# The first step's v one place earlier in the load queue, and one weight pair asked for at the state's sum

## The chip, the cores and the metric

The kernel runs on one core of one Trainium2 chip. The metric is the device time of one execution in microseconds; the median of several runs is compared. Five engines work side by side, each through its own list of instructions in order: TensorE (PE; its weight loads are listed apart as PEld), VectorE (DVE), ScalarE (ACT), GpSimd (POOL), and SyncE (SP), which here only starts DMA transfers.

## The reference

Two blocks follow each other. The first is a recurrent attention over 768 time steps, for 4 batches and 8 heads of dimension 48:

```
for t in range(S):
    cur = einsum('bhd,bhe->bhde', u * k_t, v_t)
    y[:, :, t] = einsum('bhd,bhde->bhe', r_t, state + cur)
    state = w_t[..., None] * state + einsum('bhd,bhe->bhde', k_t, v_t)
```

The second takes the result as 3072 tokens of 384 numbers and runs `h = x @ w_in` (384 to 2048), `g = h * erf(softplus(h))`, and `out = g @ w_out` (2048 to 384). The weights `w_in` and `w_out` come as 64-bit floats; everything else is 32-bit.

## The kernel before

The sequence is cut into chunks of 128 tokens, and two batches go together, so there are 12 steps (6 chunks times 2 batch pairs). In every step the attention of the chunk is computed in six levels. At each level TensorE multiplies blocks of k and r (`level_products`, L554), VectorE multiplies r and k by running products of the decay w (`scale`, L323 and L330), and the block's result is taken into a tile `own` (L564, or L571 on ScalarE at level 6). Then `from_own` (L586) multiplies `own` with v into the PSUM tile `y`, `state_part` (L661) makes k times v, `through_state` (L612) adds what comes from the carried state, and the chunk's output is copied to `xT`. The second block of an earlier step is interleaved: `hidden` (L1021) makes the products with `w_in` in pieces, each of which ScalarE copies out of PSUM (L1030, two PSUM buffers `m`), and `project` multiplies with `w_out`.

The weights are converted on the chip, in the first three steps. They are cut into 16 pairs: 0 to 7 of `w_in`, 8 to 15 of `w_out`. Each pair is loaded as 32-bit words into one of three buffers named `words` (two DMAs, L147), scaled by ScalarE twice (high words L257 or L259, low words L265), shifted by VectorE (L274), and finished by an addition on GpSimd (L287). Piece n of the first hidden layer needs pair n. The functions are kept in a table by letter: "l" load, "b" and "r" ScalarE's two scalings, "h" the shift, "o" the addition, "j" shift and addition. `done` counts how far each letter has come, and the table `CONVERT` lists, by step and level, which letters are sent: the first string of an entry before the level's result is taken, the second after it.

The order of every engine's list is the order in which the program is written (a manual schedule). When a load may start is set by a gate: a one-element copy into the buffer that is about to be loaded, which reads something that comes late enough. The DMA then waits for the copy. The copy runs on GpSimd (L242) or, where told so, on ScalarE (L240). All these loads are started by SP, in order, so a load whose gate is closed holds back everything behind it.

Two places matter here. In step 0, at level 2 of `attend_first`, SP gets pair 1's load with a gate (L800), then the first step's v (L801), then step 1's w (L802). v is read by `from_own(0, own, 1)`. In step 1, the state after step 0 is made late, in `pending()`: `state_part` on TensorE, then VectorE's two additions into `S_next` (L854). It leaves `S_next` in `turns["gate"]`, and the next load without a gate of its own takes it from there. That is pair 5's load, sent after level 2 by `("j", "brl")`; by then pair 3's shift and addition ("j") have been sent, so on GpSimd the gate copy stands behind pair 3's addition. Behind pair 5 SP has step 2's r and k (`load_halves(loaded[2][0], rkw[2])`), then pairs 6 and 7.

Of the kernel before, what the change touches and what calls it, by code (L numbers as in the profile page):

```python
# [61 lines left out]
def kernel(  # L62
# [14 lines left out]
    nc = tc.nc  # L77
# [51 lines left out]
    turns = {"next": 0}  # L129

    def products(shape, n=None):


        if n is not None:
            return ps_p.tile(shape, FP32, name=f"pp{n}")
        n = turns["next"]
        turns["next"] = 1 - n
        return ps_p.tile(shape, FP32, name=f"pp{n}")
# [5 lines left out]
    def load_halves(dst, src):  # L144

        for i in range(2):
            nc.sync.dma_start(out=dst[:, i], in_=src[:, i])  # L147
# [71 lines left out]
    def convert(weights):  # L219

        held = {}
        plain = weights[0][1].dtype == FP32
        signed = len(weights) // 2

        def load(i, behind=None, by_scalar=False):
            if i >= len(weights):
                return
            dst, src = weights[i]  # L230
            if plain:
                nc.sync.dma_start(out=dst, in_=src)
                return
            words = wide.tile([P, 2, DM, 2], I32, name="words", bufs=3)
            if behind is None:
                behind = turns.pop("gate", None)
            if behind is not None:
                to = words[:, 0, 0, 0:1].bitcast(FP32)
                if by_scalar:
                    nc.scalar.copy(to, behind)  # L240
                else:
                    nc.gpsimd.tensor_copy(out=to, in_=behind)  # L242
            load_halves(words[:].rearrange("p i n two -> p i (n two)"), src.bitcast(I32))
            held[i] = {"words": words}

        def scale_high(i, part=slice(0, 2)):


            if i not in held:
                return  # L250
            if i < 2:
                base = ps_m.tile([P, NP * C], FP32, name="m")[:, :DM]
            else:
                base = y[:].rearrange("p e q j t -> p e (q j t)")[:, :, :DM]
            high = held[i]["words"][:, part, :, 1].bitcast(FP32)
            if i < signed:
                nc.scalar.activation(base, high, AF.Prelu, scale=2.0**-112, alpha=-(2.0**32))  # L257
            else:
                nc.scalar.mul(out=base, in_=high, mul=2.0**-112)  # L259
            held[i].setdefault("bases", []).append((base.bitcast(I32), part))  # L260

        def scale_low(i):
            if i in held:
                rest = wide.tile([P, 2, DM], I32, name="rest", bufs=2)
                nc.scalar.mul(  # L265
                    out=rest[:], in_=held[i]["words"][:, :, :, 0].bitcast(U32), mul=2.0**-29
                )
                held[i]["rest"] = rest

        def shift(i):  # L270
            if i in held:
                base, part = held[i]["bases"].pop(0)
                into = weights[i][0].bitcast(I32)[:, part]
                nc.vector.tensor_scalar(  # L274
                    out=into if i < signed else base, in0=base, scalar1=3, scalar2=None,
                    op0=ALU.logical_shift_left,
                )
                if i >= signed:
                    nc.vector.scalar_tensor_tensor(
                        out=into, in0=held[i]["words"][:, part, :, 1], scalar=-(1 << 31),  # L280
                        in1=base, op0=ALU.bitwise_and, op1=ALU.bitwise_or,
                    )

        def add(i):
            if i in held:
                into = weights[i][0].bitcast(I32)
                nc.gpsimd.tensor_tensor(  # L287
                    out=into, in0=into, in1=held.pop(i)["rest"][:], op=ALU.add
                )

        def join(i):
            shift(i)
            add(i)

        stages = {"l": load, "b": scale_high, "r": scale_low, "h": shift, "o": add, "j": join}
        done = {"l": 5, "b": 2, "r": 2, "j": 2}

        def send(what):
            for stage in what:
                stages[stage](done[stage])  # L300
                done[stage] += 1

        return stages, send
# [10 lines left out]
    def scale(s, level, batch=None):  # L314

        in_t, tots = loaded[s][0], ready[s][1]
        half, nb = 1 << (level - 1), JP * C >> level
        if batch is not None:
            nb //= NJ
            halves = view(  # L320
                turns["first"][:, batch], half, [[NP * C - half, 2], [2 * half, nb], [1, half]]
            )
            nc.vector.tensor_mul(  # L323
                halves, halves,
                view(tots[level - 1], 2 * batch * nb, [[1, 2], [2, nb], [0, half]]),
            )
            return
        n = 1 if s > DIRECT and level == LOG else 2
        halves = view(in_t[:, 0:2], half, [[JP * C - half, n], [2 * half, nb], [1, half]])
        nc.vector.tensor_mul(  # L330
            halves, halves, view(tots[level - 1], 0, [[1, n], [2, nb], [0, half]])
        )
# [193 lines left out]
    def parts_of(s):  # L526

        c, i = divmod(s, SPC)
        in_t, vt = loaded[s]
        made, tots, tot = ready[s]  # L530
        ends = tot.rearrange("p (n h) -> p n h", h=NC)
        return c, in_t, vt, made, states[i][c % 2], states[i][1 - c % 2], ends
# [9 lines left out]
    def level_products(pp, rk, level, ns=range(NJ * NP)):  # L542

        half = 1 << (level - 1)
        m = HC if level <= MASKED else half
        for n in ns:
            for s0 in range(0, C, HC):
                for e in range(NE):
                    right = rk(0, n)[rows(e), s0 : s0 + HC]
                    to = pp[s0 : s0 + m, e, n, :]  # L550
                    if level > 1:
                        right = rights(right, half)
                        to = to[:, : HC // 2].rearrange("p (b h) -> p b h", h=half)
                    nc.tensor.matmul(  # L554
                        to, lhsT=rk(1, n)[rows(e), s0 : s0 + m], rhs=right,
                        start=True,
                        stop=True,
                    )
# [189 lines left out]
    def attend_first(xT):  # L748
# [5 lines left out]
        c, _, vt, made, S, S_next, ends = parts_of(0)  # L754
# [25 lines left out]
        behind = {3: (3,), 4: (4, 5), 5: (6,)}  # L780
        for level in range(2, LOG):
            pp = turns.pop("pp", None) or products([P, NE, JP, HC])
            for j, half in enumerate(halves):
                level_products(pp, first_pair, level, half)
                scale(0, level, batch=j)
            turns["pp"] = products([P, NE, JP, HC])
            keep_busy(turns["pp"], (DM,))
            take_level(own, pp, level)
            wait_for(1 << level - 1)
            if level == 2:  # L790
                totals(2, part=slice(batch // 2, batch))
            else:
                totals(*behind[level])
            if level == 2:
                stages["b"](0, 0)
                stages["b"](0, 1)
                stages["r"](0)
                for _ in prepare(1):
                    pass
                stages["l"](1, own[:, 0, 2:3])  # L800
                nc.sync.dma_start(out=vt[:], in_=v[0])  # L801
                nc.sync.dma_start(out=ws[1][:], in_=rkw[1][:, 2])  # L802
        totals = plan_totals(1)
        pp = turns.pop("pp")
# [45 lines left out]
        def pending():  # L850
            part = products([P, NE, JP, HC], turns["next"])[:, 0]
            state_part(0, kT, ps + [[part] * NE], (1,))
            for e in range(NE):
                nc.vector.tensor_add(S_next[rows(e)], faded[1][rows(e)], part[rows(e), :, :D])  # L854
            load_third()
            turns["gate"] = S_next[:, 0, 0:1]

        turns["pending"] = pending

# [364 lines left out]
    def run_late(s, tokens, following=None):  # L1224
# [26 lines left out]

    CONVERT = (
        (),
        (("j", "br"),) + (("j", "brl"),) * 4 + (("j", "l"), ("", ""), ("", ""), ("", "brl")),
        (("", "jbrl"),) * 4 + (("", "jl"), ("", ""), ("", ""), ("", ""), ("", "br")),
        (("", "jbr"), ("j", "br"), ("j", "")),
    )
# [19 lines left out]
    with tc.manual_schedule(  # L1277
# [3 lines left out]
        for t in (*states[0], *states[1], middle):  # L1281
# [3 lines left out]
        stages, send = convert(  # L1285
            [
                (into[:, f : f + 2, :], given[:, f : f + 2, :])
                for into, given in ((w_in_sb, w_in), (w_out_sb, w_out))
                for f in range(0, NT, 2)
            ]  # L1290
        )
# [165 lines left out]
```

## Time and profile before

| | us |
|---|---|
| median of 3 runs | 595.64 (592.7 to 596.28) |
| the profiled execution | 595.89 |
| its span | 594.1 |
| TensorE busy | 581.4 |
| VectorE busy | 436.7 |
| ScalarE busy | 360.8 |
| GpSimd busy | 272.8 |

The mean granted TensorE clock of the profiled execution is 0.996 of full speed. The kernel moves 63.24 MB in all; the loads of the first 60 us, weights and step inputs, take most of the DMA engines' time there.

A row of the timeline has the start and the duration in us, the engine, the source line, the operation, what it writes and reads, how many instructions are merged in the row, and in brackets how long the engine was idle before it and what ended that. "issue" means that the profile shows nothing that the engine waited for. SPq rows are DMA starts in SP's queue. A row by windows has the stretch, the sum, the busy time and the number of instructions of PE, PEld, DVE, ACT and POOL, then the granted clock, the busy share of the DMA engines and GB/s.

### The profile page before, as it was taken

The numbers are of one execution on the slowest core, as the hardware profiler recorded it, in microseconds if no ns is written. First come the engines' busy times: TensorE is split into PE (matmuls) and PEld (weight loads), VectorE is DVE, ScalarE is ACT, GpSimd is POOL, SyncE is SP. The second block draws the span as 40 slices with busy tenths as digits, with TensorE's granted clock in tenths as the row PEclk, the third lists the DMA queues.
The fourth block names the chain that finished last, engine by engine and source line by source line (L and its number), as shares of the span: only waits on it lengthen the run. The fifth ranks groups of instructions, "written<-read, shape, count | busy, mean of one in ns | idle before, by whom it ended". The sixth has DMA issues, their size and how long they took to land.

```text
span 594.1 us, 16635 instructions
## 1 busy us (share of the span) xinstructions
PE 581.4 (98%) x7256; PEld 499.1 (84%) x7256; DVE 436.7 (73%) x523; ACT 360.8 (61%) x474; POOL 272.8 (46%) x308
## 2 busy tenths in 40 slices
PE   8797999999999999999999999999999999999997
PEld 6586887678668767898898898898898898898997
DVE  7685696899996899799799799799799525023140
ACT  4536877726534497666666666666666664746710
POOL 4566263700488559649459459459459000000000
PEclk9998999999999999999999999999999999999999
DMA  7668362541324414334334334333331300000000
GB/s 243 196 211 332 114 237 88 217 143 19 142 51 151 81 77 159 72 108 169 72 108 169 73 108 168 73 108 133 73 108 53 73 8 28 2 20 15 1 26 28
DMA packets 54081, 63.24 MB, mean 106 GB/s; under 512 B 35160, under 2 KB 40568, under 8 KB 52984
## 3 DMA queue, kind: packets, MB, share of 16 engines
q1 hardware_dynamic: 53624, 61.98, 32.9%
q8 instruction: 57, 0.93, 0.7%
q10 hardware_dynamic: 384, 0.20, 0.1%
q14 instruction: 16, 0.13, 0.1%
HBM read 52.39 MB, written 8.69 MB: 103 GB/s over the span
## 4 chain that ended last, share of the span: by engine, by line
PE 60%; ACT 3%; issue 1%; DVE 1%; ACTq 0%; DVEq 0%
PE m L1129 28%; PE m L1021 27%; PE pp L554 2%; PE y L586 1%; PE y L612 1%; PE pp L661 1%; ACT room L977 1%; ACT L981 1%; ACT L977 1%; PE pp L1129 0%; ACTq L647 0%; ACT pp L981 0%; DVE in L330 0%; ACT y L981 0%; PE pp L674 0%
## 5 line engine op out<-in xcount | busy, mean ns | idle before, releaser
L1021 PE MATMUL m<-xT,w_in_sb 128*128 128x256 f32 x1152 | 259.1, 383 | 3.9 <-ACT h L1030 3.5
L1021 PEld LDWEIGHTS m<-xT,w_in_sb 128*128 128x128 f32 x1152 | 217.3, 191 | 35.8 <-issue 4.3
L1030 ACT COPY h<-m 128x512 f32<-128x512 f32 x96 | 55.4, 579 | 84.1 <-PE m L1021 84.0
L330 DVE TENSOR_TENSOR in<-in,tot_sb 128x1024 f32<-128x1024 f32 (+1 forms) x55 | 77.5, 1409 | 17.2 <-PE pp L554 13.7
L465 POOL TENSOR_TENSOR rk<-words 128x528 f32<-128x528 f32 (+3 forms) x28 | 42.5, 1516 | 92.1 <-DVE sums L455 81.7
L469 POOL TENSOR_TENSOR words<-words,rest 128x528 f32<-128x528 f32 (+10 forms) x77 | 78.2, 1015 | 6.0
L1053 PE MATMUL m<-w_out_sb,h 128*128 128x384 f32 x192 | 64.3, 491 | 0.0
L1053 PEld LDWEIGHTS m<-w_out_sb,h 128*128 128x128 f32 x192 | 35.7, 190 | 23.5
L1129 PE MATMUL m<-mixed,h 128*128 128x192 f32 x288 | 51.1, 331 | 0.0
L977 ACT ACT_TABLE_LOAD x36 | 46.2, 1283 | 3.0 <-issue 2.4
L1129 PE MATMUL m<-w_out_sb,h 128*128 128x192 f32 x272 | 47.5, 329 | 0.0
L1129 PEld LDWEIGHTS m<-mixed,h 128*128 128x128 f32 x288 | 46.6, 190 | 0.9
L981 ACT ACT_TABLE_LOAD x36 | 46.2, 1283 | 1.6 <-DVE room L1112 1.1
L1129 PEld LDWEIGHTS m<-w_out_sb,h 128*128 128x128 f32 x272 | 44.3, 190 | 0.4
L1129 PE MATMUL m<-w_out_sb,room 128*128 128x192 f32 x256 | 44.2, 326 | 0.0
L554 PEld LDWEIGHTS pp<-in 48*64 48x64 f32 (+1 forms) x2368 | 33.4, 126 | 11.8 <-issue 4.6
L1129 PEld LDWEIGHTS m<-w_out_sb,room 128*128 128x128 f32 x256 | 42.0, 190 | 0.0
L986 DVE TENSOR_TENSOR h<-h,y 128x1024 f32<-128x1024 f32 x17 | 20.7, 1215 | 28.3 <-ACT y L981 28.1
L404 POOL TENSOR_TENSOR tot_sb<-tot_sb 128x256 f32<-128x256 f32 (+4 forms) x50 | 36.9, 737 | 3.8
L977 ACT ACTIVATE room<-h 128x1024 f32<-128x1024 f32 x36 | 38.1, 1058 | 0.4
L986 DVE TENSOR_TENSOR h<-h,pp 128x1024 f32<-128x1024 f32 x19 | 23.1, 1214 | 19.7 <-ACT pp L981 19.7
L554 PE MATMUL pp<-in 48*64 48x32 f32 (+1 forms) x2368 | 37.1, 212 | 0.3 <-DVE in L330 0.2
(146 smaller groups left out, 823.4 us busy)
## 6 DMA issues: line engine op xcount, KB each, us to landing
in<-in_rkw SPq DMA_DIRECT2D x8, 1024.0 KB, 5.0
words<-in_moe_w_in SPq DMA_DIRECT2D x16, 384.0 KB, 6.9
words<-in_moe_w_out SPq DMA_DIRECT2D x16, 384.0 KB, 4.4
words<-in_rk_rows SPq DMA_DIRECT2D x8, 768.0 KB, 5.8
w<-in_rkw SPq DMA_DIRECT2D x11, 512.0 KB
v<-in_v SPq DMA_DIRECT2D x12, 384.0 KB, 5.6
out<-o SPq DMA_DIRECT2D x23, 192.0 KB, 2.8
in<-in_rkw SPq DMA_DIRECT2D x7, 512.0 KB, 6.0
```

The costliest lines, as they stand in the source:

```text
L330: nc.vector.tensor_mul(halves, halves, view(tots[level - 1], 0, [[1, n], [2, nb], [0, half]]))
L404: nc.gpsimd.tensor_mul(new, pair[:, :, 0], pair[:, :, 1])
L465: engine.tensor_mul(terms[n], r[:, :, n:], k[:, :, : near - n])
L469: engine.tensor_mul(k[:, :, :m], k[:, :, :m], w[:, :, n : n + m])
L554: nc.tensor.matmul(to, lhsT=rk(1, n)[rows(e), s0 : s0 + m], rhs=right, start=True, stop=True,)
L977: nc.scalar.activation(sp_room, chunks[0], AF.Softplus)
L981: nc.scalar.activation(at, sp_room, AF.Erf)
L986: nc.vector.tensor_mul(h, h, at)
L1021: nc.tensor.matmul(ps[:, ff, :], lhsT=w_in_sb[:, g * FG + f + ff, kk * P : (kk + 1) * P], rhs=xT[:, kk, :], start=kk == 0, stop=kk == KT - 1,)
L1030: nc.scalar.copy(h[:, f : f + FT, :], ps[:])
L1053: nc.tensor.matmul(ps[j][:], lhsT=gs[g][:, f, j * C : (j + 1) * C], rhs=w_out_sb[:, g * FG + f, :], start=g + f == 0, stop=g == NG - 1 and ...
L1129: nc.tensor.matmul(to, lhsT=a[:, f], rhs=b[:, f], start=start and f == 0, stop=f == FG - 1, skip_group_check=True,)
```

## The change

Two things move. In step 0, v's load is written ahead of pair 1's load. In step 1, pair 5's load is written into `pending()`, right after the two additions that make `S_next`, with `S_next` as its gate; the gate's hand-over through `turns` goes, and "l" goes from the entry that sent it, with `done["l"]` starting at 6 in its place. On GpSimd the gate copy of pair 5 now stands ahead of pair 3's addition instead of behind it. On SP v stands ahead of pair 1's two DMAs; the rest of SP's order, and the orders of TensorE, VectorE and ScalarE, are as they were.

```
             words = wide.tile([P, 2, DM, 2], I32, name="words", bufs=3)
-            if behind is None:
-                behind = turns.pop("gate", None)
             if behind is not None:
...
-        done = {"l": 5, "b": 2, "r": 2, "j": 2}
+        done = {"l": 6, "b": 2, "r": 2, "j": 2}
...
+                nc.sync.dma_start(out=vt[:], in_=v[0])
                 stages["l"](1, own[:, 0, 2:3])
-                nc.sync.dma_start(out=vt[:], in_=v[0])
                 nc.sync.dma_start(out=ws[1][:], in_=rkw[1][:, 2])
...
             load_third()
-            turns["gate"] = S_next[:, 0, 0:1]
+            stages["l"](5, S_next[:, 0, 0:1])
...
-        (("j", "br"),) + (("j", "brl"),) * 4 + (("j", "l"), ("", ""), ("", ""), ("", "brl")),
+        (("j", "br"),) * 2 + (("j", "brl"),) * 3 + (("j", "l"), ("", ""), ("", ""), ("", "brl")),
```

## The prediction

> **What bounds the kernel now.** I read the busy shares first, then who TensorE (PE) waited for in the first 65 us, then the timeline there, then the clock in half-microsecond slices.
>
> ```profile
> PE 581.4 (98%) x7256; PEld 499.1 (84%) x7256; DVE 436.7 (73%) x523; ACT 360.8 (61%) x474; POOL 272.8 (46%) x308
> ```
>
> PE is busy 98% of the span: 12.7 us idle in all. Cut into stretches, PE is idle 2.5 us in 0 to 21, 6.5 us in 21 to 65, 0.4 us in 65 to 232 and 3.2 us after that. So what happens before 65 us moves the end nearly one for one, if it moves PE. Who PE waited for there:
>
> ```profile
> PE m L1021 <- ACT h L1030: 3.3, 2, 2.2
> PE y L586 <- DMA v<-in_v: 1.0, 1, 1.0
> PE pp L661 <- issue: 0.9, 1, 0.9
> PE pp L554 <- issue: 0.7, 1, 0.7
> ```
>
> The largest wait is for ScalarE's copies (L1030) of hidden-layer products out of PSUM. The timeline shows why those copies are late (start, duration, engine):
>
> ```profile
> 21.91 0.66 PE L586 MATMUL y<-own,v 64*48 64x64 f32 x32 [1.02 <-DMA v<-in_v]
> 23.95 0.43 PE L661 MATMUL pp<-v,kT 64*48 64x48 f32 x11 [0.94 <-issue]
> ...
> 35.31 1.11 DVE L854 TENSOR_TENSOR s<-faded,pp 48x384 f32<-48x384 f32 x2
> 37.56 1.84 POOL L287 TENSOR_TENSOR w_in_sb<-w_in_sb,rest 128x768 int32<-128x768 int32 x1 [3.26 <-DVE w_in_sb L274]
> 39.34 1.19 POOL L242 COPY words<-s 128x1 f32<-128x1 f32 x1
> 40.55 0.81 SPq L147 DMA_DIRECT2D words<-in_moe_w_in  x2
> 41.47 0.84 SPq L147 DMA_DIRECT2D in<-in_rkw  x2
> 42.40 1.89 SPq L147 DMA_DIRECT2D words<-in_moe_w_in  x4
> 45.03 0.87 ACT L257 ACTIVATE y<-words 128x768 f32<-128x768 f32 x1 [5.22 <-DMA words<-in_moe_w_in]
> 46.62 0.56 ACT L1030 COPY h<-m 128x512 f32<-128x512 f32 x1
> 47.34 2.83 PE L1021 MATMUL m<-xT,w_in_sb 128*128 128x256 f32 x12 [1.07 <-ACT h L1030]
> 50.81 0.85 ACT L257 ACTIVATE y<-words 128x768 f32<-128x768 f32 x1 [1.43 <-DMA words<-in_moe_w_in]
> 52.38 0.57 ACT L1030 COPY h<-m 128x512 f32<-128x512 f32 x1
> 53.10 4.51 PE L1021 MATMUL m<-xT,w_in_sb 128*128 128x256 f32 x12 [2.25 <-ACT h L1030]
> 57.54 0.66 PE L586 MATMUL y<-own,v 64*48 64x64 f32 x32
> ```
>
> Pair 5 is asked for at 40.55, after GpSimd's gate copy, which stands behind pair 3's addition. ScalarE, in order, waits 5.22 us for it at L257; the PSUM copy at 46.62 stands behind that, and PE's piece 4 waits 1.07. Pair 6 repeats it (L257 at 50.81, copy at 52.38, piece 5 waits 2.25). Then the clock halves:
>
> ```profile
> 53.00:53.50 0.50, 0.40 (x2) 0.41 (x3) 0.28 (x1) 0.50 (x1) 0.50 (x1) 1.00 0.35 49
> 54.00:54.50 0.50, 0.50 (x3) 0.41 (x2) 0.50 (x1) 0.50 (x2) 0.50 (x1) 0.50 0.55 209
> ```
>
> The third column from the end is the granted clock: 1.00, then 0.50 until about 57.2. Piece 5 takes 4.51 where the pieces at 38.49 and 42.34 took 2.86: 1.65 lost.
>
> **Part 1, the first v.** On SP, v stands behind pair 1, whose gate opens at 14.47; it issues at 16.31 and lands 5.6 us later. Moved ahead, it has no wait and issues at 10.4, right after step 1's r and k. With the same 5.6 it lands by 16.0. PE's transposes end at 20.89 and `own` at 20.18, so L586 starts near 20.9: 1.0 earlier. L661 then waits for kT (21.49, VectorE): about 21.6 for 22.4, 0.8 earlier.
> Next in line is the 0.94 "issue" gap. The Trainium skill (Runtime: NRT & Kernel Launch, Instruction fetch mechanics) says an engine fetches its code by DMA in 16 KiB blocks of 256 instructions, the crossing mostly hidden. The row speaks against "hidden": PE's unexplained gaps, at 23.95, 29.01 and 34.85, lie about 127 matmul-and-load pairs apart, a block each, and transfers run until shortly before the first two. If the block's arrival were fixed, part 1 gives 0; if hidden, up to 0.8 + 0.9 = 1.7. I take that it follows the bulk traffic: v's 384 KB, about 1.0 us at the 400 GB/s of busy slices, leaves the tail before 22, so the block comes 1.0 sooner. **Value 0.9, bounds 0 and 1.7.**
> Costs: v is queued behind r and k. Should it delay them by its whole 1.0 us, ScalarE's L382 chain ends at 18.6, still before its L571 at 19.02: 0, by 0.4 us of cover. Pair 1 may land 1 us later; its reader ran at 23.32, over 8 us after issue. Step 1's w issues 0.5 earlier.
>
> **Part 2, pair 5.** No instruction is added on any engine; one copy moves on GpSimd past one addition (L287). S_next is ready at 36.42. The copy needs 0.18 (the row at 22.88, beside the same VectorE operation); its 1.19 at 39.34 ended just after VectorE's L330 (40.48), so it was held. At 36.5 GpSimd is idle (3.26 ahead of L287), and that addition needs L274, which ends at 37.42: cost 0, with 0.75 us of cover. The two DMAs issue at 36.70, 3.85 earlier. SP's order is unchanged: step 2's r and k follow, then pairs 6 and 7, whose buffers are free at 37.25 and 39.34; all move 3.85. The queue before them drains by 36.7, so I use their old latencies.
> Worked forward (times without part 1): pair 5 lands at 36.70 + 4.48 = 41.18, and L257 starts at 41.5, now behind L274 of pair 4 (ends 41.35); the copy L1030 ends at 43.66, and piece 4 follows the level-5 products at 46.20, for 47.34. VectorE's L330 waits for GpSimd's addition (45.55 to 47.37) and ends 48.45; level 6 starts at 46.20 + 2.78 = 48.98, for 50.09. Pair 6 lands 50.81 − 3.85 = 46.96; its L257, L265 and L1030 end at 49.10, so piece 5 starts at 48.98 + 0.69 = 49.67 and, at full clock, PE is through at 52.46.
> What is late next: `own`. ScalarE goes on with pair 7's L257 at 49.67 (behind L274, 49.48), L265 50.48, L1030 51.27, L571 51.73 to 52.90; so L586 at 53.05 with 0.5 us idle. **Gain 57.54 − 53.05 = 4.5.** Check: 1.07 + 2.25 + 1.65 − 0.5 = 4.5. Bounds: 2.8 (no clock gain, below) and 5.1 (no wait for `own`).
>
> Here a rule speaks against the change. The skill (TensorE: Matmul & The Clock Gate, Part 1) halves the clock after an idle window of about 3.4 us. The gap was 2.25, so by the rule it was not long enough, the dip has another cause, and 1.65 stays: 2.8. The row shows the dip 0.65 after a gap that filled most of the preceding 3.4 us, and none elsewhere from 4 to 65 us, not after gaps of 0.9 to 1.1. I go by the row: 4.5.
>
> Sum: 0.9 + 4.5 = 5.4. The profiled execution was 595.89 (span 594.1), its median 595.64; so 595.6 − 5.4 = 590.2. Later work starts from PE's results, and PE has no room from 65 to 232, so the shift carries through.
>
> **Rivals.**
> 1. Clock dip stays, the rule's way: 0.9 + 2.8 = 3.7, 591.9. Against: the row.
> 2. Part 1 is swallowed by the code block: 4.5 alone, 591.1. For: the gap has no visible releaser.
> 3. The load doesn't move, GpSimd or SP being held by something the trace doesn't show: only part 1, 594.7. Against: GpSimd's 3.26 idle, SP's queue empty.
> 4. Slower: PE's code blocks starve. Before, transfers paused from 37 to 41; now they run unbroken from 37.5 to about 48.5. The block due near level 6 is asked for about 41.9. If it waits until the queue drains (about 51 with pair 8), PE stands 2 us and pays a dip, 1.65; the piece after it again: 2 × 3.65 = 7.3 − 5.4 = +1.9, 597.5. It turns to a loss once stalls exceed 5.4 us. Against: before, that block was asked for under equal traffic and level 6 shows no gap.
>
> **Chances.** Forecast 0.60 (gain 4.6 to 6.3: 589.3 to 591.0), rival 1 0.12, rival 2 0.12, rival 3 0.05, rival 4 0.05, better than the forecast (everything hidden: 1.7 + 5.1 = 6.8, 588.8) 0.06. The range 588.6 to 593.0 leaves out rivals 3 and 4 and some scatter. A measurement here tells about 1% from none (the three runs spread 0.6%). Faster by over 1% means below 589.7, a gain of 6.0: the upper third of the forecast with the scatter, and the better case: 0.35. Slower by over 1%: 0.04.
>
> **What would show it.** L586 without a DMA wait near 20.9; the issue gap after it ends near 23.0. The gate copy ahead of pair 3's addition, 0.2 long; pair 5's issue near 35.8 (both parts), L257's 5.22 wait below 1; pieces 4 and 5 without a wait for L1030; clock 1.00 from 50 to 60; L586 of step 1 at 52.1, for 57.54. A granted clock below 1 there, or new "issue" gaps of PE between 40 and 52, would make me wrong.

## The result, and the profile after

The changed kernel takes 590.1 us (median of 17 runs, 588.9 to 592.82), the kernel before, run beside it, 593.16 (17 runs). The ratio is 0.9942 with an interval of 0.9924 to 0.9960: faster by 0.4 to 0.8%. In two later sets, each on one chip beside the kernel before, the changed kernel gave 0.9921 [0.9895, 0.9947] and 0.9936 [0.9911, 0.996]. The median falls by about 3 to 4 us. The profiled execution took 589.79 (span 588.0), 6.1 less than that of before: both times come from single executions, and the one of before had been a long one.

Lines of the code stand two lower than before, L1028 for L1030. The busy shares of the changed kernel:

```profile
PE 579.6 (99%) x7256; PEld 498.3 (85%) x7256; DVE 437.6 (74%) x523; ACT 361.2 (61%) x474; POOL 272.2 (46%) x308
```

Who TensorE waited for in the changed kernel before 65 us (total in us, times, longest), without the first row, a start-up wait of 1.7 that comes before the places in question:

```profile
PE m L1019 <- ACT h L1028: 1.2, 1, 1.2
PE pp L871 <- DVE own L562: 0.7, 2, 0.4
PE pp L552 <- DVE s L852: 0.6, 1, 0.6
```

The 3.3 of ScalarE's copies is 1.2, the wait for v and the two "issue" rows are gone, and a wait of 0.56 for the state's sum (L852) is new. The stretch from 21 to 65 us by engine, in the kernel before:

```profile
21.00:65.00 44.00, 37.49 (x806) 30.72 (x810) 25.66 (x29) 25.34 (x43) 25.98 (x25) 0.96 0.61 218
```

The same stretch in the changed kernel:

```profile
21.00:65.00 44.00, 41.22 (x951) 33.83 (x950) 31.83 (x33) 29.12 (x51) 24.83 (x25) 1.00 0.64 217
```

Between 21 and 65 us TensorE stands 2.8 instead of 6.5, at a clock of 1.00 instead of 0.96. Over the whole span its idle time falls from 12.7 to 8.4, by 4.25, and its busy time from 581.4 to 579.6, by 1.85 (the same matmuls at a higher clock): together the 6.1.

The timeline of the changed kernel around the two places:

```profile
10.45 0.43 SPq L798 DMA_DIRECT2D v<-in_v  x1
...
21.21 0.67 PE L584 MATMUL y<-own,v 64*48 64x64 f32 x32
...
27.63 2.86 PE L1019 MATMUL m<-xT,w_in_sb 128*128 128x256 f32 x12
...
35.55 0.18 POOL L240 COPY words<-s 128x1 f32<-128x1 f32 x1 [2.18 <-DVE s L852]
...
35.77 1.84 SPq L147 DMA_DIRECT2D words<-in_moe_w_in  x2
...
36.63 1.83 POOL L285 TENSOR_TENSOR w_in_sb<-w_in_sb,rest 128x768 int32<-128x768 int32 x1 [0.89 <-DVE w_in_sb L272]
...
42.41 0.91 ACT L255 ACTIVATE y<-words 128x768 f32<-128x768 f32 x1 [3.69 <-DMA words<-in_moe_w_in]
...
44.76 2.83 PE L1019 MATMUL m<-xT,w_in_sb 128*128 128x256 f32 x12
...
47.15 0.92 ACT L255 ACTIVATE y<-words 128x768 f32<-128x768 f32 x1 [0.78 <-DMA words<-in_moe_w_in]
...
49.51 2.83 PE L1019 MATMUL m<-xT,w_in_sb 128*128 128x256 f32 x12 [1.24 <-ACT h L1028]
...
52.26 0.93 PE L584 MATMUL y<-own,v 64*48 64x64 f32 x32
```

In the kernel before, piece 0 of the hidden layer stood here:

```profile
29.50 2.86 PE L1021 MATMUL m<-xT,w_in_sb 128*128 128x256 f32 x12
```

v is there when L584 starts; piece 0 comes 1.87 earlier (27.63, was 29.50). The gate copy stands ahead of pair 3's addition and takes 0.18 instead of 1.19. Pair 5 is asked for at 35.77 instead of 40.55, but ScalarE still waits 3.69 for it (5.22 before). Piece 4 has no wait, piece 5 still 1.24, and takes 2.83 for 4.51. Step 1's L584 comes at 52.26 for 57.54.

### The profile page after: what moved, and what is told of

Read it like the earlier page. It is cut to its first block, busy times and chain, and to the rows that moved or that the text cites. A ratio compares the mean times of both kernels' runs of the same rounds, so it can differ in the third digit from the quotient of the medians.

```text
span 588.0 us, 16635 instructions
## 1 busy us (share of the span) xinstructions
PE 579.6 (99%) x7256; PEld 498.3 (85%) x7256; DVE 437.6 (74%) x523; ACT 361.2 (61%) x474; POOL 272.2 (46%) x308
## 4 chain that ended last, share of the span: by engine, by line
PE 81%; DVE 9%; DMA 1%; issue 1%; ACT 1%; POOL 0%; SPq 0%; DVEq 0%; ACTq 0%; POOLq 0%
PE m L1019 37%; PE m L1127 28%; PE m L1051 6%; PE pp L552 4%; PE y L584 2%; DVE in L328 2%; PE y L610 2%; PE pp L659 1%; DMA words<-in_moe_w_in 1%; DVE words L467 1%; DVE rk L463 1%; DVE sums L453 1%; DVE h L1008 1%; DVE mixed L1075 1%; PE pp L930 1%
## 5 line engine op out<-in xcount | busy, mean ns | idle before, releaser
L1028 ACT COPY h<-m 128x512 f32<-128x512 f32 x96 | 55.7, 580 | 82.4 <-PE m L1019 82.3
L402 POOL TENSOR_TENSOR tot_sb<-tot_sb 128x256 f32<-128x256 f32 (+4 forms) x50 | 35.2, 704 | 3.8
```

The lines of the kernel that those rows point to most:

```text
L402: nc.gpsimd.tensor_mul(new, pair[:, :, 0], pair[:, :, 1])
L1028: nc.scalar.copy(h[:, f : f + FT, :], ps[:])
```

## The experiments

They ran in three sets, each on one chip beside its own runs of the kernel before, whose medians were 594.17 (32 runs), 593.87 (15) and 594.45 (24). Three questions were open: which part carries the gain, whether it is the wait or the clock, and what the "issue" gaps of TensorE are that stood behind v.

### Each part alone

Only v's load moved, in the kernel before:

```
+                nc.sync.dma_start(out=vt[:], in_=v[0])
                 stages["l"](1, own[:, 0, 2:3])
-                nc.sync.dma_start(out=vt[:], in_=v[0])
```

> v's load ahead of pair 1 alone; pair 5 stays where it was. As forecast (the code block comes with the bulk traffic): 0.9 us below the kernel before. If the two code-block gaps behind v vanish altogether: 1.7 to 1.8 below, and no 'issue' gap of PE between 22 and 30 in the trace. If the block's arrival is fixed: no gain, and the gap ends near 24 as before. In all three the wait of 2.25 us ahead of piece 5 stays.

Only pair 5's load moved: the changed kernel with v's load back behind pair 1's.

```
-                nc.sync.dma_start(out=vt[:], in_=v[0])
                 stages["l"](1, own[:, 0, 2:3])
+                nc.sync.dma_start(out=vt[:], in_=v[0])
```

> Pair 5's load at the state's sum alone; v stays behind pair 1. As forecast (the halved clock belongs to every run of the kernel before): 4.5 us below the kernel before. If the halved clock falls only on some runs of before: about 2 to 3 us below its median, with no clock below 1 in the trace, and a smaller scatter than before. PE's v wait of 1.0 us and its code gaps stay in both.

Measured side by side in the first set: v alone 593.65, ratio 0.9988 [0.9971, 1.0004]; pair 5 alone 590.97, ratio 0.9942 [0.9921, 0.9963]. In the second set the whole change and pair 5 alone ran side by side:

> The changed kernel again, beside the one with pair 5's move alone. If v's move adds on top of pair 5's: 0.7 to 1.8 us below pair 5's move alone. If v's move gives nothing even then, because GpSimd's and VectorE's chain up to S_next or pair 6's transfer sets step 1: within 0.5 us of it.

> Pair 5's move alone, again, as the partner of the changed kernel on the same chip: 2.5 to 3.5 us below the kernel before.

The whole change gave 589.9 there (0.9921 [0.9895, 0.9947]), pair 5 alone 590.53 (0.9924 [0.9895, 0.9953]). Pair 5's move has the whole measurable gain; v's adds 0.6 by the medians, which these runs can't tell from nothing.

Pair 5 alone was expected to keep the wait of 1.0 for v and the issue gaps. Its first profile has neither, with v at its old place in the queue:

```profile
21.31 0.66 PE L584 MATMUL y<-own,v 64*48 64x64 f32 x32
22.12 1.16 PE L659 MATMUL pp<-v,kT 64*48 64x48 f32 x31
28.12 2.86 PE L1019 MATMUL m<-xT,w_in_sb 128*128 128x256 f32 x12
```

So the late v and the gaps behind it, from which the prediction took part 1, come in some executions only. Of the four profiles with v at its old place (the kernel before, pair 5 alone twice, and the filled kernel below) only two have a wait for v: 1.02 and 0.21.

The timeline of v alone shows where its gain goes:

```profile
27.59 2.86 PE L1021 MATMUL m<-xT,w_in_sb 128*128 128x256 f32 x12
...
38.34 1.19 POOL L242 COPY words<-s 128x1 f32<-128x1 f32 x1
...
39.56 0.81 SPq L147 DMA_DIRECT2D words<-in_moe_w_in  x2
...
45.15 0.85 ACT L257 ACTIVATE y<-words 128x768 f32<-128x768 f32 x1 [6.34 <-DMA words<-in_moe_w_in]
...
47.42 4.51 PE L1021 MATMUL m<-xT,w_in_sb 128*128 128x256 f32 x12 [2.84 <-ACT h L1030]
```

Piece 0 comes 1.91 earlier than before (27.59 for 29.50), yet piece 4 starts at 47.42, where it started at 47.34 before. Pair 5's gate still stands behind pair 3's addition; its load is asked for 1.0 earlier (39.56), but is not there earlier. ScalarE stands 6.34 for it instead of 5.22, and TensorE, which is early, waits 2.84 ahead of piece 4 instead of 1.07; now piece 4 is the one at half clock (4.51). The expectation had the wait of 2.25 ahead of piece 5 stay; it moved to piece 4. In this execution piece 5 then has no wait, so that L586 comes at 55.34, 2.2 before the kernel before had it; the medians say 0.5, so most of those 2.2 are not typical.

The same holds with pair 5 early. Here is TensorE in another execution of the changed kernel, from the second set:

```profile
23.20 0.43 PE L659 MATMUL pp<-v,kT 64*48 64x48 f32 x11 [0.42 <-issue]
...
28.79 0.56 PE L552 MATMUL pp<-rk 48*64 48x64 f32 x18 [1.21 <-issue]
29.28 2.86 PE L1019 MATMUL m<-xT,w_in_sb 128*128 128x256 f32 x12
...
49.72 2.86 PE L1019 MATMUL m<-xT,w_in_sb 128*128 128x256 f32 x12
52.51 0.66 PE L584 MATMUL y<-own,v 64*48 64x64 f32 x32
```

The issue gaps are back, and piece 0 starts at 29.28, 1.65 later than in the first profile; but piece 5 has no wait here, and L584 comes at 52.51, only 0.25 later. A loss of this size in step 0 is mostly made up in the wait for pair 6. A larger one is not: in the second profile of pair 5 alone piece 0 starts at 31.32 and L584 at 55.25, 3.69 and 2.99 later than in the first profile of the changed kernel.

### The wait or the clock

The prediction put 1.65 of its 4.5 down to the half clock after the 2.25 gap. In the kernel before, half of piece 4's matmuls are now computed a second time, in the wait ahead of piece 5, so that the gap is split (three calls, which the trace lists as six; ScalarE's copy of that piece stands behind the repeat):

```
+                if not of and g and f == FT:
+                    for kk in range(KT):
+                        nc.tensor.matmul(
+                            ps[:, 0, :],
+                            lhsT=w_in_sb[:, g * FG, kk * P : (kk + 1) * P],
+                            rhs=xT[:, kk, :],
+                            start=kk == 0,
+                            stop=kk == KT - 1,
+                        )
+                    nc.scalar.copy(h[:, 0:FT, :], ps[:])
```

> The kernel before, with three matmuls of piece 4 run a second time in the wait ahead of piece 5 (same result, its copy out of PSUM after ScalarE's L571), so that PE is never idle for over 1.5 us there. If the halved clock comes from that wait in every run: 1.65 us below the kernel before, clock 1.00 from 50 to 60. If it falls only on some runs: the median moves by less than 0.8 us, and the slowest third of the runs by 1.65 or more. If the dip has another cause: clock 0.5 again after 53.7, no gain.

The timeline of TensorE in this filled kernel:

```profile
50.62 1.56 PE L1020 MATMUL m<-xT,w_in_sb 128*128 128x256 f32 x6
52.82 2.83 PE L1031 MATMUL m<-xT,w_in_sb 128*128 128x256 f32 x12 [0.64 <-ACT h L1041]
55.58 0.66 PE L586 MATMUL y<-own,v 64*48 64x64 f32 x32
```

The repeat (L1020) fills the gap down to 0.64, and piece 5 runs at full clock (2.83). The median is 593.52, ratio 1.0002 [0.9982, 1.0022]: no gain that can be measured. The mean clock of each run tells more. In the profiled execution of the kernel before, one stretch of 3.4 us at half clock is there (53.8 to 57.2); such a stretch lowers the mean of 590 us by 0.003, so the stretches of a run can be counted, as an estimate, from its mean clock. In the same set the kernel before had none in 7 of 32 runs and one to three in 25; the filled kernel had none in 8 of 12. So with the gap split, fewer runs have a half-clock stretch. Among the runs without one, though, the kernel before took 592.82 and the filled one 593.27: the filling itself seems to cost some 0.5. With one stretch the kernel before took 594.19, 1.4 more than without; in the other two sets the same difference is 1.1 and 0.6. Of the three outcomes expected, the second fits best, and not fully: the slowest third of the runs lies only 0.7 lower (means of 595.8 and 596.5), not 1.65.

Over all runs whose clock is on record, the kernel before has at least one stretch in 56 of 71, the changed kernel in 5 of 30, and pair 5 alone in 9 of 18. So v's move, which the medians don't show, may keep some of the stretches away; that was not tried on its own. Among runs without any, the changed kernel is faster by 2.9 us in the second set (589.86 for 592.74) and 2.1 in the third (590.37 for 592.49), from four to six runs each. That is an estimate of what the waits alone are worth; the stretches that now come rarely make up the rest of the 3 to 4.

### What TensorE's issue gaps are

Two kernels lengthen the bulk of loads ahead of the first gap, with v itself in time: loads of v into a buffer where nothing reads them, behind pair 1 in the queue, one in the first kernel and three in the second. (The recorded text of the second says ahead of pair 1; they stood behind it.)

```
                 stages["l"](1, own[:, 0, 2:3])
+                for n in range(3):
+                    nc.sync.dma_start(
+                        out=room[:, n, : NH * D].rearrange("p (n d) -> p n d", d=D), in_=v[0]
+                    )
```

> The changed kernel, with v loaded a second time at its old place into a buffer that nothing reads there, so that the queue carries as much behind pair 1 as before. If PE's gaps are code blocks that wait for bulk traffic: 'issue' gaps of 0.9 and 0.7 us come back near 23 and 28, and it is 0.9 to 1.6 us slower than the changed kernel. If only v's own lateness counted: as the changed kernel within 0.3 us.

> The changed kernel with v loaded three more times ahead of pair 1, into a buffer that nothing reads there, so that the transfers of step 0 end near 22.5 us in place of 20. If PE's 'issue' gaps are its code blocks behind bulk traffic: a gap of 0.5 us or more comes back near 22 to 24, with the same v in time. If the gaps have nothing to do with traffic: no gap, and as the changed kernel within 0.5 us.

One load more, in the first set: 589.56, 0.9931 [0.9907, 0.9956], no gap; but its transfers ended before 21 us all the same, so that it decides nothing. Three more, in the second set: 591.68, 0.995 [0.9928, 0.9972]. TensorE in that kernel:

```profile
20.85 0.66 PE L584 MATMUL y<-own,v 64*48 64x64 f32 x32
21.67 0.65 PE L659 MATMUL pp<-v,kT 64*48 64x48 f32 x20
23.98 0.43 PE L659 MATMUL pp<-v,kT 64*48 64x48 f32 x11 [1.66 <-issue]
...
29.30 0.56 PE L552 MATMUL pp<-rk 48*64 48x64 f32 x18 [0.99 <-issue]
```

Its half microseconds there (granted clock, busy share of the DMA engines and GB/s are the last three columns):

```profile
21.50:22.00 0.50, 0.35 (x18) 0.36 (x17) 0.43 (x3) 0.00 (x0) 0.17 (x2) 1.00 1.04 410
22.00:22.50 0.50, 0.32 (x15) 0.20 (x10) 0.50 (x2) 0.24 (x1) 0.13 (x2) 1.00 0.73 297
22.50:23.00 0.50, 0.00 (x0) 0.00 (x0) 0.19 (x1) 0.50 (x2) 0.17 (x1) 1.00 0.40 131
```

v is no longer waited for, and the gap is 1.66, longer than in the kernel before: it is not v's. The kernel is 1.8 us slower than the changed kernel beside it, with half clock in 7 of its 8 runs (1 of 6 for the changed kernel); the profiled run is the one without. TensorE comes to that place at about 22.3 and goes on 1 to 2 us after the bulk has passed. The same stands in the other traces. In the kernel before the bulk ended near 22.3 and TensorE went on at 23.95; in the changed kernel's first profile it ended at 19.8 and there is no gap; in its second one it ended near 21.8 and TensorE went on at 23.20. In pair 5 alone it ended near 21.2 and the rows show no gap.

What the gap is, the traces hold too. The page of every run lists a DMA queue for instructions (packets, MB, share of 16 engines; here the kernel before):

```profile
q8 instruction: 57, 0.93, 0.7%
```

These are packets of 16 KB, and the trace has 14,616 instructions of TensorE, 57 times 256 and a few. Before 65 us the "issue" gaps of all the traces stand right after 961, 1217, 1473 or 1729 instructions of TensorE's list, 256 apart; the gap of the next section stands after 705. Each ends 1.2 to 1.6 us after a packet of this queue: in the kernel before a packet ran from 21.50 to 22.47 and TensorE went on at 23.95; with three more loads from 21.63 to 22.56, and 23.98. The packet itself comes late behind the loads. Counted from TensorE's passing of the boundary at 705, it started 1.39 later in the changed kernel's first profile, 2.40 in its second, 3.41 in the kernel before and 3.51 with three more loads. So the gaps are TensorE's own code, arriving behind the bulk. This fits the blocks of 256 instructions that the Trainium skill names (Runtime: NRT & Kernel Launch, Instruction fetch mechanics); its "mostly hidden" does not hold where bulk loads run. What takes the 1.2 to 1.6 us between the packet and the next matmul is not shown.

### Earlier still

If the wait for pairs 5 and 6 is what counts, asking sooner should give the remaining 1.24, unless the denser loads starve TensorE's code. Pair 5 without a gate, sent where its buffer is free:

```
                 send("br")
+                stages["l"](5)
...
-            stages["l"](5, S_next[:, 0, 0:1])
```

> The changed kernel with pair 5's load written right behind pair 2's two reads and with no gate, so that it queues directly behind pairs 3 and 4 and step 2's w (near 30.5 in place of 35.8). If the pause of the transfers from 36 to 38 us is what makes pair 6 late for piece 5: piece 5's wait of 1.2 us goes, and 0.7 to 1.2 us below the changed kernel. If ScalarE's and VectorE's own chain sets piece 5: within 0.3 us. If the earlier bulk starves the PE's code block or the loads before it: slower by 0.5 or more, with a new 'issue' gap between 30 and 42.

In the second set it took 590.04, 0.992 [0.9895, 0.9946], against 589.9 of the changed kernel: the same. Pair 5 is asked for 4.8 earlier (30.96), and no piece waits for ScalarE. But an issue gap comes in its place, inside a level of step 1. The timeline of TensorE with pair 5 ungated:

```profile
28.66 0.56 PE L552 MATMUL pp<-rk 48*64 48x64 f32 x18 [1.08 <-issue]
...
41.76 0.55 PE L552 MATMUL pp<-in 48*64 48x32 f32 x24 [0.60 <-issue]
...
49.57 2.86 PE L1019 MATMUL m<-xT,w_in_sb 128*128 128x256 f32 x12
52.36 0.66 PE L584 MATMUL y<-own,v 64*48 64x64 f32 x32
```

L584 comes at 52.36, for 52.26 and 52.51 in the two profiles of the changed kernel. Then pair 1's gate was taken away too, alone and with pair 5's, beside the changed kernel:

```
-                stages["l"](1, own[:, 0, 2:3])
+                stages["l"](1)
```

> The changed kernel with pair 1's load without its gate, so that it queues directly behind v (near 11 in place of 14.3) and the transfers of step 0 end near 18.5 us in place of 20 to 21.5. If PE's code blocks come behind the bulk: no 'issue' gap near 23 or 28, PE's piece 0 near 27.4 in every run. If what PE gains in step 0 is taken back by piece 5's wait (pair 6), the time stays within 0.5 us of the changed kernel all the same. If gains add up: 1 to 2 us below it.

> The same, and pair 5 without a gate right behind pair 2's reads as well. Piece 5 no longer waits for pair 6, so PE's gain in step 0 should now reach step 1's end: L584 of step 1 near 51 in place of 52.3, and 1.0 to 2.0 us below the changed kernel. If it does not, step 1 is set by ScalarE's and VectorE's conversions and not by any load: within 0.5 us of the changed kernel.

> The changed kernel once more, as the partner on the same chip: 3 to 5 us below the kernel before, with a clock of 0.999 or 1.000 in four runs of five.

Pair 1 alone 592.1, 0.9971 [0.9947, 0.9994]; both 592.37, 0.9959 [0.9939, 0.998]; the changed kernel 590.63, 0.9936 [0.9911, 0.996]. By the medians both are 1.5 to 1.7 us slower than the changed kernel, though the intervals overlap a little. The timeline of TensorE with both gates gone:

```profile
17.28 0.91 PE L870 MATMUL pp<-s,ident 128*128 128x384 f32 x2
20.64 1.08 PE L552 MATMUL pp<-in 48*32 48x32 f32 x64 [2.45 <-issue]
21.65 1.65 PE L870 MATMUL pp<-s,ident 128*128 128x384 f32 x2
```

The same kernel by microseconds:

```profile
18.00:19.00 1.00, 0.20 (x1) 0.00 (x0) 0.95 (x2) 0.00 (x0) 0.35 (x2) 1.00 0.68 270
19.00:20.00 1.00, 0.00 (x0) 0.00 (x0) 0.00 (x0) 0.00 (x0) 0.00 (x0) 0.87 0.19 66
20.00:21.00 1.00, 0.36 (x27) 0.36 (x31) 0.00 (x0) 0.00 (x0) 0.00 (x0) 0.50 0.05 20
```

With pair 1 ungated the queue runs without a break into 18.5 us, and TensorE stands 2.45 at level 6 of step 0, one place earlier than before, while no engine works; the clock halves in the gap and stays so until about 26.6. A packet of instructions ran from 18.25 to 19.18, 1.46 before TensorE went on. The gaps at 23 and 28 are gone: the bulk has ended by then. But piece 0 starts at 31.80 and step 1's L584 at 55.20, where 51 had been expected. With pair 1's gate gone alone, the gap is at the same place, 1.65 long, and the profile of the changed kernel in this set has it there too, 1.14 long, as has the second one of pair 5 alone, 1.69. (Rows there name VectorE's `own`, which with pair 1 ungated had ended 0.9 before TensorE went on; the packet of instructions ended 1.47 before.) So the place is not peculiar to the ungated kernels. What goes with them is a longer gap and more half clock: in 10 of 12 runs with both gates gone and 7 of 12 with pair 1's, for 1 of 7 of the changed kernel. Without any half clock, pair 1 ungated still takes 591.26 for 590.37. No kernel tried is better than the changed one beyond the scatter.

## Why the prediction was right, and where its steps were not

The time, 590.2 forecast and 590.1 measured, and the sign were right. But that the two agree to 0.1 owes something to luck: the gain of 5.4 was worked out on one execution of 595.89 and set against a median of 595.64, from three runs. Over more runs the kernel before is at 593.2 to 594.5. Against those the gain is 3 to 4, so the sum was too large by 1.4 to 2.3 for a typical run, while in the profiled pair (6.1 less) it was too small. The profiled execution of before had the half clock, the late v and the issue gaps all at once.

**Part 1, value 0.9: the step "Sum: 0.9 + 4.5" failed.** Inside step 0 it went as said, with more: no wait for v, and an issue gap that follows the bulk, as the choice against "arrival fixed" had it; with both gaps gone piece 0 came 1.87 earlier, past the upper bound of 1.7. That was one execution: in the changed kernel's second profile the gaps are back and piece 0 is only 0.22 earlier than before (29.28), and pair 5 alone has a profile without the wait for v. The term was read off an execution in which v was late. And the two parts lie on one chain and meet at the next wait, that for pair 5 or, with pair 5 early, pair 6. v alone is worth 0.5, with no change inside its interval, and beside pair 5's move 0.6, not resolved. Rival 2 (part 1 gives nothing) was right in its result and in part in its reason: the code gap took the gain in some executions, the load that comes after in others.

**Part 2, 4.5: the mechanism was right, and it carries the whole gain.** The gate copy took 0.18 and cost pair 3's addition nothing (36.63, after L272); pair 5's issue at 35.77 was forecast as 35.8. Three terms were of the wrong size:

- The landing. "The queue before them drains by 36.7, so I use their old latencies": pair 5 took 6.64 from issue to use (35.77 to 42.41) where 4.48 was forecast. The queue had not drained: the engines still moved 155 GB/s from 35 to 36. The two DMA starts took 1.84 for 0.81, and the transfers fell to a trickle at the same time. The changed kernel by microseconds:

```profile
35.00:36.00 1.00, 0.44 (x26) 0.39 (x28) 0.97 (x2) 0.00 (x0) 0.18 (x1) 1.00 0.38 155
36.00:37.00 1.00, 1.00 (x55) 0.96 (x49) 0.97 (x2) 0.48 (x1) 0.37 (x1) 1.00 0.32 66
37.00:38.00 1.00, 1.00 (x6) 0.87 (x5) 1.00 (x2) 1.00 (x2) 1.00 (x1) 1.00 0.80 249
```

  Asked for 4.8 earlier, it reached ScalarE only 2.6 earlier than before (42.41 for 45.03). The first profile of pair 5 alone shows the same (starts 2.05, landing 6.20). It is not so in every execution: in the changed kernel's second and third profile the starts took 0.81 and 0.98, and the landing 5.04 and 5.20. So the landing was taken too short by 0.6 to 2.2. What makes the starts long was not tried. The sign "L257's 5.22 wait below 1" did not follow from the working, which leaves 1.7 (41.5 less 39.81, the end of ScalarE's copy before it); it was 3.69.
- What is late next. Forecast: no wait ahead of piece 5, 0.5 for `own`. Measured: 1.24 ahead of piece 5, since pair 6 was waited for until 47.15 (forecast 46.1 with part 1), and 0.3 for `own`, inside L584 (0.93 long for 0.66). The errors nearly cancel: L584 at 52.26, forecast 52.1.
- The clock, 1.65. It came in full in the profiled execution: 1.00 from 14 to 66 us. As a term of a typical run it was too large: the half clock is a matter of chance, which the change moves from 56 of 71 runs to 5 of 30. The rule weighed there (TensorE: Matmul & The Clock Gate, Part 1: an idle window of about 3.4 us) would leave the 1.65 where it was; with the gap split, the half clock was absent from 8 of 12 runs (7 of 32 in the kernel before), so the gap of 2.25 did have to do with it. But 4 of 12 runs had it all the same, and the median moved by only 0.65, inside its interval. Neither the row nor the rule is a yes or no here; what decides in a single run stays open.

**The rivals.** Rival 1's gain, 3.7, is nearest to the fall of the medians, though its time of 591.9 stood on the old median and its clock that stays is not what the runs show. Rival 3 fell with the issue at 35.77. Rival 4 did not come about: the changed kernel's first profile has no issue gap between 40 and 52. Its mechanism is real all the same: where the loads were made denser, gaps of 0.6 (pair 5 without gate) and 2.45 with a half clock (both without gate) came, and the two kernels with pair 1 ungated are slower than the changed one by the medians.

## What to carry to other kernels

Savings on one chain don't add: follow the earlier one to the next wait, and count only what passes it. Work out a gain against one execution, and state it against many: if the profiled run shows a dip of the clock, a late load or gaps without a releaser, profile it again before they are counted, since part of the gain may be luck that the median doesn't have. A gap marked "issue" can be the engine's own code: look for the packets of the instruction queue. Before a load is asked for earlier, see what runs in the queue at that time: a gate that leaves a break between bulk loads can be worth more than the head start.

## What the runs showed of the hardware

TensorE's "issue" gaps, 0.3 to 2.45 us long, stand 256 instructions apart and end 1.2 to 1.6 us after a 16 KB packet of the instruction queue. Behind bulk loads this packet started up to 3.5 us after TensorE had passed the boundary before, and 1.4 us after it where the bulk had ended by 19.8.

The clock was halved for 3.4 to 6.8 us after or in gaps of 1.69 (pair 5 alone, in its second profile), 2.25, 2.45 and 2.84, but not after gaps of 1.65 and 1.66, and not in every run of the same kernel.

Pair 5's two DMA starts took 0.80 or 0.81 us on SP in the three profiles where the DMA engines were idle before (the kernel before, v alone, the filled kernel). Where earlier loads were still running they took 0.80 to 2.05, so that busy engines alone don't set it.
